# One copy moved to ScalarE, a new order of attention units between half output steps, and partial sums in buffers of their own

## The chip, the cores and the metric

The program runs on one core of a Trainium2 chip. The metric is the device time of one execution in microseconds (us); a profile's span, from its first to its last instruction, is about 1.8 us shorter. The machine prints with every execution the mean clock that was granted to TensorE. Here that number matters more than usual: executions of one and the same kernel fall into a group at a mean clock of 0.998 to 1.000, called full-clock or fast below, and one at 0.966 to 0.993, called slow. Comparisons of kernels below are between full-clock executions, where a kernel has any. Where a recorded ratio includes a lower clock, this is said, and the ratio without it, a plain ratio of mean times, is given beside it. That the slow group is made by these kernels themselves is shown by experiments that provoke it (5: a gap of 3.40 us, four of four executions at a clock of 0.966 to 0.986) and remove it (6: the gap filled, six of six at 0.998 to 1.000).

## The reference

Per head, an 8x8 matrix P is made from `sort_net` by five rounds of exp, row and column normalisation. P mixes the blocks of k and of v, attention runs inside each block of 96 rows, and the result goes through a bilinear FFN.

```python
k_sorted = einsum('bhij,bhjcd->bhicd', P, k_b)        # 4 x 8 heads, 8 blocks of 96, D = 64
v_sorted = einsum('bhij,bhjcd->bhicd', P, v_b)
scores = scale * q_b @ k_sb.T
attn = exp(scores - max); attn /= attn.sum(-1) + 1e-9
x = (attn @ v_sb) as (3072, 512)
out = ((x @ w_a) * (x @ w_b)) @ w_out                 # d_ff = 1536
```

## The kernel before

Heads are handled in pairs, four pairs to a batch; g counts the pairs. "c" mixes k and v of a pair, "s" makes its scores, "o" its outputs. These units of batch b+1 are spread between the FFN steps of batch b. The prologue does the first halves of batch 0 alone. These are the parts that the argument touches (cuts marked `...`):

```python
load_q(0); make_identity(...); load_q(1)              # all of these are issued by GpSimd, in this order
for hp in range(HP): load_pair(0, hp)
load_ab(0); load_ab(1)                                # weights
...
replicate(nc.vector, 0)                               # p_rep: P repeated along the row, first half
replicate(nc.gpsimd, 1)                               # second half: behind the loads above on GpSimd
to_columns(0)                                         # TensorE: p_rep -> pc_ps
spread(...); spread(...)
load_ab(2); load_ab(3)
half_mix(0, 0, "k", "act", fill=2, cols=256)          # fill: dummy matmuls that keep TensorE busy
half_mix(0, 0, "v", "dve")
to_columns(1)                                         # needs the second half of p_rep
half_mix(0, 1, "k", "act")
...
begun = [psF.tile([P, 512], FP32, tag="F", name="pf") for _ in range(3)]
two = psA.tile([P, 2, 512], FP32, tag="A", name="two")
begun += [two[:, 0], two[:, 1]]                       # five partial FFN sums, two of them in one tile
...
def o_(g):
    stage_o(g); to_xT(g)
    if 2 * HP <= g + 2 < B * HP:
        pair_q(g + 2); stage_q(g + 2)                 # GpSimd copy, then a transposing DMA
for n in range(HP + 1):                               # order c0 s0 c1 s1 o0 c2 s2 o1 c3 s3 o2 o3
    if n < HP: us.append(c_(g0 + n)); us.append(s_(g0 + n))
    if n > 0:  us.append(o_(g0 + n - 1))
...
steps = [(1, f) for f in ab] + [(2, f) for f in po]   # an output step: 12 matmuls, weight 2
```

The softmax here doesn't subtract the row's maximum and nothing guards it: scores larger than these inputs give would overflow.

## Time and profile before

| | |
|---|---|
| time, three executions | 252.80, 252.12, 252.27 us |
| span of the profiled execution, mean clock | 251.9 us, 0.973 |
| TensorE busy, share of the chain that ended last | 241.9 us, 89% |

The page of before: first the header, then busy time and share of TensorE, then the clock granted in 40 slices of 6.3 us, in tenths.

```profile
span 251.9 us, 5520 instructions
PEclk9965799999999999999999999999999999999999
```

The third to fifth slices are the only ones below full clock. The view by windows of 1 us shows it in detail; its columns are the window, its length, then busy time with counts of PE (TensorE's matmuls), PEld (its weight loads), DVE (VectorE), ACT (ScalarE) and POOL (GpSimd), then the granted clock, and last the DMA share and GB/s.

```profile
13.00:14.00 1.00, 0.00 (x0) 0.00 (x0) 0.42 (x1) 0.15 (x1) 0.78 (x2) 1.00 1.31 206
14.00:15.00 1.00, 0.09 (x3) 0.09 (x4) 0.00 (x0) 0.00 (x0) 1.00 (x3) 0.78 1.33 199
15.00:16.00 1.00, 1.00 (x24) 0.78 (x24) 0.42 (x1) 0.30 (x1) 0.90 (x2) 0.50 1.36 196
28.00:29.00 1.00, 1.00 (x10) 0.57 (x8) 0.00 (x0) 0.00 (x0) 0.70 (x1) 0.90 1.45 196
```

TensorE does nothing from 13 to 14 us, and its clock is halved just after. The clock record of the trace has a low stretch of 13.65 us there. Why TensorE stands still is in the timeline (start, length, engine, line, operation, count, and in brackets the idle time before it and what ended it). TensorE of before:

```profile
12.26 0.38 PE L180 MATMUL mixh<-s_all,k 128*64 128x64 bf16 x12
12.44 0.38 PE L180 MATMUL mixh<-s_all,v 128*64 128x64 bf16 x12
14.91 0.28 PE L441 MATMUL pc_ps<-ident,p_rep 32*128 32x32 bf16 x4 [2.09 <-POOL p_rep L435]
15.13 0.54 PE L180 MATMUL mixh<-s_all,k 128*64 128x64 bf16 x12
...
32.80 0.32 PE L332 MATMUL two<-xT,w_a_sb 128*128 128x384 bf16 x1 [0.60 <-DVE hT L353]
...
77.28 0.34 PE L302 MATMUL sc<-qTf,kT 64*128 64x96 bf16 x8 [0.65 <-ACT kT L162]
77.80 0.35 PE L302 MATMUL sc<-qTf,kT 64*128 64x96 bf16 x8 [0.17 <-ACT vT L162]
84.71 0.65 PE L231 MATMUL o_ps<-vs,eT 96*128 96x65 bf16 x16 [0.79 <-DMA vs<-vT]
```

GpSimd of before, which TensorE waits for at 14.91:

```profile
9.80 0.71 POOL L95 DMA_DIRECT2D v<-in_v_dram  x1 [1.64 <-DMA q_first<-in_q_dram]
...
13.71 0.74 POOL L106 DMA_DIRECT2D w_b_sb<-in_moe_w_b_dram  x1 [0.22 <-issue]
14.45 0.41 POOL L435 COPY p_rep<-p_fin 32x256 f32<-32x256 f32 x1
```

The p_rep copy takes 0.41 us, but it stands in line behind DMA issues. The twelve mixing matmuls at 15.13 take 0.54 us where the same number took 0.38 at 12.26: that is the half clock. The other waits of TensorE are small: one at 32.80 for VectorE's reading of the other half of "two", and three in batch 0's output steps at 77 to 85 us.

### The profile page before, as it was taken

Reading aid. Unit: us, or ns where it says so; the run is one execution under the profiler, and the core shown is the slowest. Engines: PE = TensorE matmul, PEld = TensorE weight load, DVE = VectorE, ACT = ScalarE, POOL = GpSimd, SP = SyncE. Lnnn points to the kernel's source line nnn. Section 1 sums busy time; section 2 is a strip of 40 time slices with the busy share of each in tenths; the row PEclk is TensorE's granted clock in tenths of the full one; section 3 lists DMA queues with packets and bytes.
Section 4 is the critical chain, followed back from the end, with each engine's and each line's share of the span. In section 5 each row is a group of like instructions: output and inputs, shape, how many; then the busy total and the mean of one; then the engine's idle time right before and its main releaser. Section 6 shows DMA issues by size and latency. Waiting matters only on the chain.

```text
span 251.9 us, 5520 instructions
## 1 busy us (share of the span) xinstructions
PE 241.9 (96%) x2258; PEld 140.3 (56%) x2258; DVE 109.7 (44%) x259; ACT 104.3 (41%) x203; POOL 60.9 (24%) x88
## 2 busy tenths in 40 slices
PE   7869999999998899999999999999999999999995
PEld 2446566666654446565654456565655455666443
DVE  6735355754742424454543324363624244444110
ACT  3534475366445016555543045636342033333101
POOL 8686468610205103505051012510000000000000
PEclk9965799999999999999999999999999999999999
DMA  6999999944497997666668768645223410000123
GB/s 82 199 199 197 196 201 182 192 69 23 85 150 130 191 169 122 84 110 97 104 99 183 156 142 134 109 76 62 54 54 113 141 61 0 0 3 1 42 94 114
DMA packets 53129, 27.82 MB, mean 110 GB/s; under 512 B 29936, under 2 KB 50160, under 8 KB 53104
## 3 DMA queue, kind: packets, MB, share of 16 engines
q0 software_dynamic: 20944, 14.16, 40.1%
q1 hardware_dynamic: 32016, 13.25, 24.6%
q8 instruction: 17, 0.28, 0.5%
q10 hardware_dynamic: 144, 0.07, 0.1%
q14 instruction: 8, 0.07, 0.1%
HBM read 28.32 MB, written 6.29 MB: 137 GB/s over the span
## 4 chain that ended last, share of the span: by engine, by line
PE 89%; DMA 6%; POOL 2%; DVE 1%; ACT 0%; issue 0%
PE pf L332 50%; PE po L375 22%; PE mix L281 4%; PE o_ps L231 3%; DMA k<-in_k_dram 3%; DMA vs<-vT 3%; PE sc L302 2%; PE mixh L180 2%; PE vs_ps L208 1%; PE sc L195 1%; PE po L362 1%; PE xt_ps L222 1%; PE mixh L168 1%; PE two L332 1%; PE q_ps L260 1%
## 5 line engine op out<-in xcount | busy, mean ns | idle before, releaser
L353 DVE TENSOR_TENSOR hT<-a_sb,pf 128x384 bf16<-128x384 bf16 x95 | 52.6, 554 | 74.3 <-PE pf L332 48.4
L332 PE MATMUL pf<-xT,w_a_sb 128*128 128x384 bf16 x380 | 78.3, 328 | 0.0
L332 PE MATMUL pf<-xT,w_b_sb 128*128 128x384 bf16 x380 | 77.8, 327 | 0.0
L352 ACT CAST a_sb<-pf 128x384 bf16<-128x384 f32 x95 | 45.5, 479 | 62.1 <-PE pf L332 40.8
L375 PE MATMUL po<-w_out_sb,hT 128*128 128x512 bf16 x276 | 61.7, 379 | 0.0
L332 PEld LDWEIGHTS <-w_b_sb 128*128 128x128 bf16 x384 | 37.7, 98 | 25.5 <-DMA w_b_sb<-in_moe_w_b_dram 0.6
L332 PEld LDWEIGHTS <-w_a_sb 128*128 128x128 bf16 x384 | 35.0, 98 | 22.4 <-issue 0.3
L375 PEld LDWEIGHTS <-hT 128*128 128x128 bf16 x276 | 26.3, 98 | 30.3
L162 ACT COPY o_sb<-po 128x512 f32<-128x512 f32 (+1 forms) x13 | 7.5, 578 | 51.0 <-PE po L375 49.5
L164 DVE COPY o_sb<-po 128x512 f32<-128x512 f32 (+1 forms) x12 | 7.9, 658 | 44.3 <-PE po L375 38.7
L307 ACT ACTIVATE eT<-sc 96x768 bf16<-96x768 f32 x24 | 18.1, 803 | 3.2 <-PE sc L302 3.2
L533 POOL COPY gate<-kT 1x1 bf16<-1x1 bf16 x8 | 1.4, 180 | 72.8 <-ACT kT L162 72.8
L237 DVE TENSOR_TENSOR xp<-o_ps,rec 96x512 bf16<-96x512 f32 x24 | 15.7, 683 | 0.2
L162 ACT CAST kT<-mix 128x384 bf16<-128x384 f32 x24 | 10.3, 483 | 8.1 <-PE mix L281 8.1
L231 PEld LDWEIGHTS <-eT 96*128 96x128 bf16 x256 | 11.1, 102 | 3.7 <-issue 1.3
L95 POOL DMA_DIRECT2D v<-in_v_dram x16 | 11.5, 718 | 5.5 <-DMA w_b_sb<-in_moe_w_b_dram 2.5
L231 PE MATMUL o_ps<-vs,eT 96*128 96x65 bf16 x256 | 12.0, 199 | 0.8 <-DMA vs<-vT 0.8
L95 POOL DMA_DIRECT2D k<-in_k_dram x16 | 11.6, 724 | 4.5 <-PE pf L332 2.3
L246 POOL COPY qc<-q 128x768 bf16<-128x768 bf16 x9 | 7.5, 831 | 16.9 <-DMA q<-in_q_dram 16.9
L95 POOL DMA_DIRECT2D q<-in_q_dram x12 | 8.6, 713 | 1.4 <-DMA w_b_sb<-in_moe_w_b_dram 0.6
L164 DVE CAST vT<-mix 128x384 bf16<-128x384 f32 x12 | 6.7, 558 | 3.8 <-PE mix L281 3.8
L168 PE MATMUL heat<-warm 128*128 128x512 bf16 x21 | 6.9, 467 | 1.3 <-DVE warm L77 1.3
(80 smaller groups left out, 159.2 us busy)
## 6 DMA issues: line engine op xcount, KB each, us to landing
out_dram<-o_sb SPq DMA_DIRECT2D x17, 256.0 KB, 2.0
k<-in_k_dram POOLq DMA_DIRECT2D x16, 192.0 KB, 5.0
v<-in_v_dram POOLq DMA_DIRECT2D x16, 192.0 KB, 6.7
q<-in_q_dram POOLq DMA_DIRECT2D x12, 192.0 KB, 6.3
w_a_sb<-in_moe_w_a_dram POOLq DMA_DIRECT2D x6, 256.0 KB, 10.1
w_b_sb<-in_moe_w_b_dram POOLq DMA_DIRECT2D x6, 256.0 KB, 11.2
w_out_sb<-in_moe_w_out_dram POOLq DMA_DIRECT2D x3, 512.0 KB, 10.3
out_dram<-o_sb SPq DMA_DIRECT2D x12, 128.0 KB, 2.4
```

Of the source, the lines that this page charges most:

```text
L95: nc.gpsimd.dma_start(out=to, in_=_ap(t, base, [[W, P], [S * D, 2], [1, W]]))
L162: nc.scalar.copy(out=out, in_=in_)
L164: nc.vector.tensor_copy(out=out, in_=in_)
L168: nc.tensor.matmul(ps[:, 0:cols], lhsT=warm[:, 0:P], rhs=warm[:, 0:cols], start=True, stop=True)
L231: nc.tensor.matmul(o_ps[:, e, i * (D + 1):(i + 1) * (D + 1)], lhsT=eT[:, hf, e, i * BLK:i * BLK + P], rhs=vs[0:BLK, i0 + i, V0 - 1 + e * ( ...
L237: nc.vector.tensor_tensor(out=_ap(xp, i0 * 2 * D, [[nxp * 2 * D, BLK], [D, 2], [2 * D, NBH], [1, D]]), in0=_ap(o_ps, 1, [[1024, BLK], [511 ...
L281: nc.tensor.matmul(mix[e * D:(e + 1) * D, c // 3, c % 3 * P:(c % 3 + 1) * P], lhsT=src2[:, e, c * D:(c + 1) * D], rhs=s_all[:, 2 * g + e], ...
L307: nc.scalar.activation(out=eT[:, hf, :, 0:HB], in_=sc[0:BLK, :, 0:HB], func=AF.Exp, scale=float(scale))
L332: nc.tensor.matmul(pf[:, 0:HW], lhsT=w_sb[:, kc, m * P:(m + 1) * P], rhs=x_cols(b, kc, t), start=(kc == 0), stop=(kc == KA - 1))
L352: nc.scalar.copy(out=a_sb, in_=pf[:, 0:HW])
L353: nc.vector.tensor_mul(out=hT[:, m, t * HW:(t + 1) * HW], in0=a_sb, in1=ab[1][:, 0:HW])
L375: nc.tensor.matmul(po, lhsT=hT[:, m, c * P:(c + 1) * P], rhs=w_out_sb[:, m, :], start=(m == 0), stop=(m == KO - 1))
```

## The change

Its intent: take the copy out of GpSimd's line; let no two units share an FFN step by cutting an output step in halves; give the transposing DMA of v more time by mixing a pair before the output of the pair two back; stage q of the next pair at the scores, because the new order would leave too little time otherwise; and end the false sharing of "two". The core of the diff (cuts marked):

```diff
-            replicate(nc.vector, 0)
-            replicate(nc.gpsimd, 1)
+            replicate("dve", 0)
+            replicate("act", 1)
...
-            two = psA.tile([P, 2, 512], FP32, tag="A", name="two")
-            begun += [two[:, 0], two[:, 1]]
+            begun += [psA.tile([P, 2, 512], FP32, tag="A", name="two")[:, 0] for _ in range(2)]
...
     def ffn_out(b, c):
...
+        def part(n):
+            if n == 0:
+                held["po"] = psF.tile([P, DMODEL], FP32, tag="F", name="po")
+            for m in range(n * KO // 2, (n + 1) * KO // 2):
+                nc.tensor.matmul(held["po"], lhsT=hTs[b][:, m, c * P:(c + 1) * P],
+                                 rhs=w_out_sb[:, m, :], start=(m == 0), stop=(m == KO - 1))
+            if n == 1:
+                store(b, c, held["po"])
+        return [lambda: part(0), lambda: part(1)]
...
             def s_(g):
...
+                if 2 * HP <= g + 1 < B * HP:
+                    pair_q(g + 1)
+                    stage_q(g + 1)
             def o_(g):
                 stage_o(g)
                 to_xT(g)
-                if 2 * HP <= g + 2 < B * HP:
-                    pair_q(g + 2)
-                    stage_q(g + 2)
...
+            for u, n in ((c_, 0), (s_, 0), (c_, 1), (s_, 1), (c_, 2), (o_, 0), (s_, 2), (c_, 3),
+                         (o_, 1), (s_, 3), (o_, 2), (o_, 3)):
+                us.append(lambda u=u, g=g0 + n: u(g))
...
-            steps = [(1, f) for f in ab] + [(2, f) for f in po]
+            steps = ab + po
```

More of the change, by code (lines that the diff above doesn't have):

```diff
@@ L369, in ffn_out, with store @@
         if b == B - 1 and c == NCH - 1:
-            ffn_last(b, c)
-            return
-        hT = hTs[b]
-        po = psF.tile([P, DMODEL], FP32, tag="F", name="po")
-        for m in range(KO):
-            nc.tensor.matmul(po, lhsT=hT[:, m, c * P:(c + 1) * P], rhs=w_out_sb[:, m, :],
-                             start=(m == 0), stop=(m == KO - 1))
+            return [lambda: ffn_last(b, c)]
+        held = {}
+        def part(n):
[7 more added lines that the diff above has]
+        return [lambda: part(0), lambda: part(1)]
+    def store(b, c, po):
         o_sb = ffp.tile([P, DMODEL], FP32, tag="o_sb", name="o_sb", bufs=3)
@@ L434, in replicate @@
             def replicate(eng, hf):
-                eng.tensor_copy(
-                    out=p_rep[:, hf * NR:(hf + 1) * NR],
-                    in_=_ap(p_fin, hf * NR, [[NB * NB, BH], [1, NR], [0, CG // 2]]))
+                copy(eng, p_rep[:, hf * NR:(hf + 1) * NR],
+                     _ap(p_fin, hf * NR, [[NB * NB, BH], [1, NR], [0, CG // 2]]))
             def to_columns(hf):
@@ L545, in o_ @@
                 to_xT(g)
-                if 2 * HP <= g + 2 < B * HP:
-                    pair_q(g + 2)
-                    stage_q(g + 2)
-            for n in range(HP + 1):
-                if n < HP:
-                    us.append(lambda g=g0 + n: c_(g))
-                    us.append(lambda g=g0 + n: s_(g))
-                if n > 0:
-                    us.append(lambda g=g0 + n - 1: o_(g))
+            for u, n in ((c_, 0), (s_, 0), (c_, 1), (s_, 1), (c_, 2), (o_, 0), (s_, 2), (c_, 3),
+                         (o_, 1), (s_, 3), (o_, 2), (o_, 3)):
+                us.append(lambda u=u, g=g0 + n: u(g))
             return us
@@ L567, in paced @@
         def paced(ab, po, units, spare):
-            steps = [(1, f) for f in ab] + [(2, f) for f in po]
-            total = sum(t for t, f in steps) - 2 * spare
-            now = done = 0
-            for t, step in steps:
+            steps = ab + po
+            total = len(steps) - 2 * spare
+            done = 0
+            for now, step in enumerate(steps, 1):
                 step()
-                now += t
                 while done < len(units) and done * total < now * len(units):
@@ L585 @@
                   for m in range(KO) for t in range(2) if b > 0 or t == 1]
-            po = [lambda c=c, b=b: ffn_out(b, c) for c in range(NCH)]
+            po = [f for c in range(NCH) for f in ffn_out(b, c)]
             paced(ab, po, units_full(b + 1) if b + 1 < B else [], 3 if b == 0 else 2)
```

## The prediction

> **What bounds the kernel.** The page has TensorE busy for 241.9 of 251.9 us, and 89% of the chain that ended last. From 34 us the timeline shows groups at their repeating pace (8 matmuls of 128x384 in 1.30 us, 12 of 128x512 in 2.59 us) with almost nothing between. To win: its idle time and slow clock:
>
> 1. At 12.82 us TensorE stops for 2.09 us until GpSimd's p_rep copy lands. The copy takes 0.41 us, but GpSimd starts it at 14.45, behind four weight-load issues; p_fin was done at 11.23.
> 2. The windows view gives a granted clock of 0.50 from 14.6 to 28.2 us. Twelve mixing matmuls take 0.46 us there, 0.24 us at full clock. [...] the gap as cause is inference.
> 3. At 32.2 us, 0.60 us: the last matmul of begun[4] waits for VectorE's read of begun[3], in the same tile "two".
> 4. In batch 0's output stage two units share one step: scores follow their mix at once (0.65 + 0.17 us waiting for kT and vT copies), and the last o waits 0.79 us for vs<-vT, 6.8 us in landing.
> Batches 1 and 2 show no TensorE idle.
>
> **What the change does.**
> - Replication on ScalarE: it is free from 11.62 us (after two qT copies) until 12.67. A 256-column copy is about 0.40 us (estimate from 479 ns for 384 columns). Ready near 12.05, before TensorE asks at 12.82. Gap 1 goes: -2.1 us, all on the chain; k of pair 1 had landed at 12.47.
> - Clock: [...] Stepping through the prologue at full clock with the trace's durations (last v near 17.4, ScalarE and VectorE about 2 us a pair), the FFN starts near 21 us instead of 26.6. If the clock drops later anyway, near 23-24. Extra gain 0 to 4 us; I take 2.3.
> - Own buffers: -0.6 us. The next scores tile takes begun[3]'s buffer, free by then.
> - Half-output steps and new order: in batch 0 no two units share a step; the last mix moves from the first output step to the eleventh of twelve a/b steps, so vs has about 9 us. -1.6 us. Batches 1 and 2 keep the same pacing: about 0.
> - q staged one pair ahead instead of two: about 8 us for a 0.83 us copy and a 2.8 us transpose: 0.
>
> Sum: 2.1 + 2.3 + 0.6 + 1.6 = 6.6, less 0.4 for new small waits: 6.2 us.
>
> **Prediction: 246.1 us, 8 in 10 between 243.5 and 248.8.** Faster by over 2% (below 247.2): 0.66; within 2%: 0.33; slower: 0.01.
>
> **What would show each step.** Timeline: p_rep on ACT ending near 12.1, no gap before the second pc_ps group, first pf matmul at 21 to 24 us. Windows: [...] at best no 0.50 at all. No wait of begun[4] on hT. At 70-85 us no TensorE wait on kT, vT or vs. Batches 1 to 3 of equal length.
>
> **What would make it wrong.** The clock falling anyway: [...] then 248-249. [...] Or late weights, q copies blocking the GpSimd or SyncE queue, psA waits between c and o.

## The result, and the profile after

| | executions, us | median |
|---|---|---|
| before, first three | 252.80, 252.12, 252.27 | |
| before, three beside the kernel after | 246.99, 247.71, 247.06 | 249.92 of all six |
| after, six | 245.78, 246.03, 246.22, 245.48, 245.97, 246.53 | 246.00 |

Ratios are the mean time of one kernel's fast runs over that of the other's of the same rounds, so not quite the ratio of the medians. Here that is 0.9949, 95% interval 0.9925 to 0.9974: half a per cent, the same at the 2% mark. The forecast of the absolute time, 246.1, was hit; the forecast of the change was not. The kernel before has executions near 247.2 too, and the prediction had been reckoned from one near 252.3. The hit is luck in part: from before's slow mean (252.40) to its fast mean (247.25) it is 5.1 us, where the prediction put 4.4 on gap and clock, and from there to after 1.25 us, where it put 1.8 on the rest. The two errors nearly cancel.

The page of after has no slice below full clock:

```profile
span 244.0 us, 5508 instructions
PEclk9999999999999999999999999999999999999999
```

TensorE of after, at the places shown of before:

```profile
12.15 0.38 PE L180 MATMUL mixh<-s_all,k 128*64 128x64 bf16 x12
12.34 0.38 PE L180 MATMUL mixh<-s_all,v 128*64 128x64 bf16 x12
12.66 0.26 PE L448 MATMUL pc_ps<-ident,p_rep 32*128 32x32 bf16 x4
12.85 0.38 PE L180 MATMUL mixh<-s_all,k 128*64 128x64 bf16 x12
...
17.12 0.30 PE L195 MATMUL sc<-qT,kT 64*128 64x96 bf16 x6
18.24 0.22 PE L195 MATMUL sc<-qT,kT 64*128 64x96 bf16 x2 [0.82 <-issue]
...
26.20 0.34 PE L332 MATMUL two<-xT,w_a_sb 128*128 128x384 bf16 x1
...
70.08 0.72 PE L302 MATMUL sc<-qTf,kT 64*128 64x96 bf16 x16
75.72 0.42 PE L231 MATMUL o_ps<-vs,eT 96*128 96x65 bf16 x8 [0.17 <-DVE xp L237]
```

ScalarE of after, with the copy that GpSimd did:

```profile
11.18 0.40 ACT L162 COPY p_rep<-p_fin 32x256 f32<-32x256 f32 x1
```

The gap is gone, the wait at "two" is gone (26.20 has no bracket), and of the waits at 77 to 85 us one of 0.17 us is left, of another kind. One thing is new: at 18.24 TensorE has stood still for 0.82 us, and "issue" means that the profile shows nothing it waited for.

The comparison that counts is with a full-clock execution of before. The kernel before was therefore run again and profiled (experiment 1); its TensorE at the same places:

```profile
13.50 0.26 PE L441 MATMUL pc_ps<-ident,p_rep 32*128 32x32 bf16 x4 [0.66 <-POOL p_rep L435]
...
18.50 0.22 PE L195 MATMUL sc<-qT,kT 64*128 64x96 bf16 x2 [0.23 <-issue]
...
27.14 0.32 PE L332 MATMUL two<-xT,w_a_sb 128*128 128x384 bf16 x1 [0.61 <-DVE hT L353]
...
71.63 0.34 PE L302 MATMUL sc<-qTf,kT 64*128 64x96 bf16 x8 [0.65 <-ACT kT L162]
72.14 0.35 PE L302 MATMUL sc<-qTf,kT 64*128 64x96 bf16 x8 [0.17 <-ACT vT L162]
72.64 2.54 PE L375 MATMUL po<-w_out_sb,hT 128*128 128x512 bf16 x11 [0.16 <-issue]
78.43 0.65 PE L231 MATMUL o_ps<-vs,eT 96*128 96x65 bf16 x16 [0.17 <-DMA vs<-vT]
```

In this execution the gap is 0.66 us instead of 2.09, and the wait for vs is 0.17 instead of 0.79. Its GpSimd shows why the gap is shorter:

```profile
8.38 0.71 POOL L95 DMA_DIRECT2D v<-in_v_dram  x1 [0.23 <-DMA q_first<-in_q_dram]
...
13.04 0.41 POOL L435 COPY p_rep<-p_fin 32x256 f32<-32x256 f32 x1
```

The v load was held up for 0.23 us, not 1.64, and everything that GpSimd does after it, the copy included, comes 1.4 us earlier. The packet records of the traces fit this: each load ends with sixteen 4-byte packets. For the second q load these lie within 0.4 us of each other in the fast execution. In the slow one fifteen come by 6.60 us after the first issue and the last at 7.96; the v load that waits for q starts 8.55 us after that issue, behind the last packet, and every later load up to 10 us has its last one behind in the same way. Why one of the sixteen trails in some executions stays open.

From the two fast traces the 1.6 us between the spans (245.6 and 244.0) divide as follows:

| stretch | before, fast | after | difference |
|---|---|---|---|
| start of the span to the first FFN matmul | 21.71 us | 21.45 us | -0.26 |
| from there to the first mix of batch 1's stage | 66.38 us | 64.98 us | -1.40, of which "two" 0.61 |
| from there to the end | 157.5 us | 157.5 us | 0.0 |

### The profile page after: what moved, and what is told of

The parts are those of the page before. It is cut to its first block, busy times and chain, and to the rows that moved or that the text cites. A ratio compares the mean times of both kernels' runs of the same rounds, so it can differ in the third digit from the quotient of the medians.

```text
span 244.0 us, 5508 instructions
## 1 busy us (share of the span) xinstructions
PE 236.7 (97%) x2246; PEld 137.3 (56%) x2258; DVE 109.6 (45%) x259; ACT 104.6 (43%) x204; POOL 60.6 (25%) x87
## 4 chain that ended last, share of the span: by engine, by line
PE 94%; DVE 3%; issue 1%; ACT 1%
PE pf L332 52%; PE po L377 24%; PE mix L281 4%; PE o_ps L231 3%; PE sc L302 2%; PE heat L168 2%; PE mixh L180 2%; PE po L362 1%; PE vs_ps L208 1%; PE sc L195 1%; PE xt_ps L222 1%; PE q_ps L260 1%; PE two L332 1%; DVE xp L237 1%; DVE o_sb L164 0%
## 5 line engine op out<-in xcount | busy, mean ns | idle before, releaser
L231 PEld LDWEIGHTS <-eT 96*128 96x128 bf16 x256 | 10.3, 97 | 3.2 <-DVE xp L237 0.6
L235 DVE RECIPROCAL rec<-o_ps 96x8 f32<-96x8 f32 x32 | 5.6, 189 | 14.0 <-PE o_ps L231 14.0
L231 PE MATMUL o_ps<-vs,eT 96*128 96x65 bf16 x256 | 11.3, 193 | 0.2 <-DVE xp L237 0.2
```

What stands on the lines that cost most here:

```text
L231: nc.tensor.matmul(o_ps[:, e, i * (D + 1):(i + 1) * (D + 1)], lhsT=eT[:, hf, e, i * BLK:i * BLK + P], rhs=vs[0:BLK, i0 + i, V0 - 1 + e * ( ...
```

## The experiments

All gave correct results. Each job also ran the kernel before in the same rounds. Jobs, each on another chip: experiments 1 to 4, 5 to 8, 9 to 12, 13 to 15.

**1. The kernel before, again.** No edit. Theory A puts the low clock of some executions down to the 2.09 us gap.

> The kernel before, unchanged, to find what its two groups of times (246.99 to 247.71 and 252.12 to 252.8 us) are. Theory A [...]: both groups can appear; an execution near 247 has a granted clock of 1.00 through 14 to 28 us although the gap of about 2 us is still there, and one near 252 or more has about 13.6 us of half clock. Theory B (a slower chip or session, nothing to do with the gap): all runs of this job lie in one group and the kernel after, or parts of it, are slow with it. Under A a fast profile has a span near 245 us and starts its FFN near 22 to 22.5 us.

Measured: five executions, 247.19 to 247.63 us, clock 0.999 to 1.000. Beside it, before ran 12 times on the same chip: nine at 246.88 to 247.59 (clock 0.999 or 1.000) and three at 252.13 to 253.34 (clock 0.973 to 0.980). Both groups come on one chip in one job, which theory B does not allow. The FFN starts at 21.71, a little earlier than expected. The gap is there, but it is not "about 2 us": it is 0.66, so the expectation was wrong in this, and the two profiled executions differ in the gap itself.

**2. Only the replication on ScalarE.**

```diff
-            replicate(nc.gpsimd, 1)
+            replicate("act", 1)
```

> Before plus only the replication on ScalarE. Theory A: no execution of the slow group; clock 1.00 throughout; p_rep on ACT done before 12 us and no gap. Theory A1 (the gap counts in full at full clock too): 245.0 us, 2.1 below the fast runs of before. Theory A2 (at full clock the prologue after the gap is bound by arriving v and weights and by ScalarE and VectorE, so the gap is mostly hidden): 246.5 to 247.3, under 0.6 below the fast runs of before. Theory B: as often slow as before.

Measured: 246.65 to 248.57 us, six executions, all at full clock; ratio 1.0011 (0.9987 to 1.0035). No slow one, as theory A says. The gap is gone in the trace and yet there is no gain over before's fast runs, so theory A1 falls. A2 is nearer, but four of the six executions lie above its range, and the cause that it names is not what the traces show in the end (below). The executions lie in groups at 246.7, 247.7 and 248.6; the profiled one is of the lowest, 246.70.

**3. The kernel after, with the replication back on GpSimd.**

```diff
-            replicate("act", 1)
+            replicate(nc.gpsimd, 1)
```

> The kernel after with the replication back on GpSimd. Theory A: the gap is back, so executions in a slow group 5 to 6 us above its fast ones may appear; its fast ones under A1 at 248.1 (after plus 2.1), under A2 at 246.0 to 246.5. Theory B: no slow group unless all kernels of the job are slow.

Measured: four of seven at full clock, 245.75 to 246.89 us; three at 250.65 to 250.97 with clock 0.973 to 0.979. The profile caught a slow one: a gap of 2.04 us and 10.24 us of half clock from 14.8 us. With GpSimd back the slow group is back. The fast executions are as fast as after's, so the gap again costs little at full clock.

**4. Only the half steps, the new order and the staging of q.** The parts of the diff from `ffn_out` on.

> Before plus the split output steps, the new order of units and the staging of q at the scores; tile 'two' and GpSimd replication as before. From the traces of before and after, batch 0 from the first FFN matmul is 1.35 us shorter by this part: fast runs 245.5 to 245.9, and in the trace no TensorE wait of more than 0.2 us between 65 and 80 us. If the gain is lost in waits elsewhere: 246.5 to 247.1. Slow executions under theory A as in before.

Measured: four fast at 246.35 to 246.39 us, one slow at 251.73; ratio 0.9965 (0.9952 to 0.9979), so about 0.9 us. From the first FFN matmul to batch 1's first mix it takes 65.66 us against 66.38, so 0.72 us and not 1.35. The 1.35 had come from the slow trace, whose wait for vs was longer; the largest wait left between 65 and 80 us is 0.18 us.

**5. The gap made long in every execution.** Two dummy copies on GpSimd ahead of the replication.

```diff
+            nc.gpsimd.tensor_copy(out=w_out_sb[:, 8:10], in_=_ap(warm, 0, [[512, P], [0, 2], [1, 512]]))
+            nc.gpsimd.tensor_copy(out=w_out_sb[:, 10, 0:256], in_=warm[:, 0:256])
             replicate(nc.gpsimd, 1)
```

> Before, with two dummy GpSimd copies (about 1.4 us together, estimate from 0.83 us for a 768-column copy) ahead of the GpSimd replication, so that the gap is about 2.1 us in every execution and not only where the second q load lands late. Theory A (the idle gap lets the clock fall): all or nearly all executions slow, 251.5 to 254 us, with 10 to 14 us of half clock from about 14.6 us. Theory C (the late load itself, or something that comes with it, lowers the clock, and the gap is a bystander): mostly 248.5 to 249, clock 1.00, and slow only as often as before (3 of 12).

Measured: 254.34, 251.38, 255.00 and 254.37 us, clock 0.966 to 0.986 in all four. The profile:

```profile
16.31 0.28 PE L441 MATMUL pc_ps<-ident,p_rep 32*128 32x32 bf16 x4 [3.40 <-POOL p_rep L435]
```

The gap was 3.40 us, since this execution also had the late q load, and 13.65 us of half clock follow it. Before kept its clock in five of 11 executions of this job, this kernel in none of four.

**6. The gap filled with dummy matmuls.** The copy stays on GpSimd, as late as it is.

```diff
             half_mix(0, 0, "v", "dve")
+            keep_busy(heat[:, 0], 8)
             to_columns(1)
```

> Before, with 8 dummy matmuls of 512 columns (1.73 us at full clock, from 0.216 us each) put into the gap ahead of the second pc_ps group; GpSimd still replicates, as late as ever. Theory A: no slow execution at all; executions with the early q load 0.6 to 1.1 us over before's fast ones (248.0 to 248.5), those with the late load 0.3 to 1.4 over (247.7 to 248.8); clock 1.00. Theory C: still slow executions near 252 to 254.

Measured: 248.07 to 249.46 us, six executions, none slow, clock 0.998 to 1.000. Its profile is one with the late q load, and its p_rep copy starts at 14.30 us:

```profile
13.21 1.90 PE L168 MATMUL heat<-warm 128*128 128x512 bf16 x8
15.05 0.26 PE L441 MATMUL pc_ps<-ident,p_rep 32*128 32x32 bf16 x4
```

A late load, a late copy, no idle TensorE, and no loss of clock. With experiment 5 this settles theory A against theory C: here it is TensorE's idleness that costs the clock, and not the late load.

**7. After, with q staged behind o again.**

```diff
             def s_(g):
-                if 2 * HP <= g + 1 < B * HP:
-                    pair_q(g + 1)
-                    stage_q(g + 1)
             def o_(g):
+                if 2 * HP <= g + 2 < B * HP:
+                    pair_q(g + 2)
+                    stage_q(g + 2)
```

> The kernel after with only the staging of q put back behind o, two pairs ahead. In the new order o of a pair comes right before the scores two pairs on, so q of those scores is asked for one FFN step (about 1.4 us) or two before it is used, against 0.83 us copy plus 2.8 us transpose. If the move was needed: TensorE waits on qTf of 1 to 3 us at up to 8 places, 250 to 256 us. If other slack covers it: 245.8 to 246.5.

Measured: 257.60 to 260.44 us, worse than expected. The profile has four waits, and with three of them goes a stretch of 3.41 us at half clock:

```profile
113.82 0.81 PE L302 MATMUL sc<-qTf,kT 64*128 64x96 bf16 x16 [2.25 <-DMA qTf<-qc]
130.33 0.52 PE L302 MATMUL sc<-qTf,kT 64*128 64x96 bf16 x16 [2.48 <-DMA qTf<-qc]
177.07 0.51 PE L302 MATMUL sc<-qTf,kT 64*128 64x96 bf16 x16 [2.80 <-DMA qTf<-qc]
191.43 0.52 PE L302 MATMUL sc<-qTf,kT 64*128 64x96 bf16 x16 [1.96 <-DMA qTf<-qc]
```

The low stretches begin at 113.87, 130.94 and 192.38 us. The longest wait, 2.80 us, is the one without, so the length of a wait alone does not decide. The stretches in the clock records of the traces have lengths that are multiples of 3.413 us: 3.41 here, 10.24 in experiment 3, 13.65 and 225.28 in before, 238.93 in after; that the clock goes in such steps is my estimate from these lengths. Counted in such steps from the end of the second low stretch, that wait is the only one that a step's border (175.31 us) cuts into 1.04 and 1.76 us; the other three lie each within one step.

So the move of the staging gains nothing by itself, but the new order can't do without it.

**8. The kernel after, again.** No edit.

> The kernel after, unchanged, beside before on one chip. Theory A: no slow execution in any round, 245.4 to 246.6, clock 1.00, whatever before does; over all executions the mean gain is the fast gain of about 1.3 us plus about 5 us times before's share of slow executions. Whether the spread of 1 us is again the late q load (the second q landing 7.0 instead of 5.6 us after its issue) the trace may show if it catches one.

Measured: 245.43 to 246.54 us, six executions, all at full clock. Before, beside it: five of 11 at full clock (247.14 to 247.87), one at 249.37 with clock 0.986, five at 251.42 to 252.90. Ratio of the fast runs 0.9927 (0.9889 to 0.9965); this set of before includes the one at 249.37. Without it the ratio is 0.9942, which agrees with the first result. The profiled execution (246.54) had an early q load; its p_fin came 0.70 us later than in the first profile of after (245.78), so nearly all of the 0.76 us between the two comes from the end of the softmax chain and not from q.

**9. Only the two buffers.**

```diff
-            two = psA.tile([P, 2, 512], FP32, tag="A", name="two")
-            begun += [two[:, 0], two[:, 1]]
+            begun += [psA.tile([P, 2, 512], FP32, tag="A", name="two")[:, 0] for _ in range(2)]
```

> Before plus only the two partial tiles in buffers of their own. The 0.61 us wait of the last begun[4] matmul on the hT product goes, in early and late executions alike: fast executions 246.7 to 246.9 beside 247.3 of before, slow ones still there at 251.5 to 253 as often as before. If the wait only moves to the next scores tile: 247.3.

Measured: three fast at 246.69 to 246.84, as expected; three slow at 250.85 to 251.75. Ratio 0.9963 (0.9937 to 0.9990). The profile is of a slow one with an early q load and a gap of only 0.96 us:

```profile
13.68 0.26 PE L441 MATMUL pc_ps<-ident,p_rep 32*128 32x32 bf16 x4 [0.96 <-POOL p_rep L435]
```

So a gap of 0.96 us can be enough, where 0.66 and 0.75 us (experiments 1 and 4) were not. Where the gap lies bears on this too. In steps of 3.413 us (the estimate of experiment 7), counted back from the fall, the step before the fall is 11.34 to 14.75 us; it holds the whole gap, and TensorE was busy in it for 2.23 us. In experiments 1 and 4 the step with the gap had 2.75 and 2.67 us busy. Over the prologues of all profiles with a clock record, the clock fell after the steps with 0.02 to 2.23 us busy and after none with 2.5 us or more. That is no general rule: in experiment 7 a step amid FFN matmuls with 1.65 us busy (175.31 to 178.72) kept the clock. No experiment moved the steps against a fixed gap.

**10. Only the output steps in halves, with their pacing; old order.**

> Before plus only the output steps in halves with their pacing; order of units and staging of q as before. By the trace of before's fast execution the waits of scores on kT and vT (0.65, 0.17 and 0.16 us) come from two units in one step; they go with the split alone, so fast executions 246.3 to 246.7, as good as split, new order and q staging together (246.37). If the new order is what gains: 247.0 to 247.4, with a wait of o on vs<-vT of 1 us or more.

Measured: fast 247.36 to 247.42; three others at 249.48 to 253.88 with clock 0.971 to 0.986. No gain: the main expectation was wrong, and its alternative, 247.0 to 247.4 with a longer wait for vs, came true. The profile is of a slow execution; set beside the slow one of before, the waits of the scores on kT and vT are gone, but the last o waits 1.39 us where it waited 0.79:

```profile
83.64 0.65 PE L231 MATMUL o_ps<-vs,eT 96*128 96x65 bf16 x16 [1.39 <-DMA vs<-vT]
```

Half steps, new order and staging of q belong together: the half steps alone gain nothing (10), and the new order without the staging loses some 12 us (7). The new order without the half steps was not run.

**11. Only the replication, once more.** As experiment 2.

> The replication alone once more, for the two groups within its fast executions (246.65 to 246.70 and 247.66 to 248.57). Theory D: the groups are the early and the late second q load; [...] and its FFN starts about 1 us later than 21.2 us at clock 1.00. Theory E: the groups come from something else (the start of the softmax chain, instruction fetch); a profile near 247.7 then shows the load complete early.

Measured: 246.83 to 247.41 us, six executions, all at full clock; ratio 0.9976 (0.9955 to 0.9997). The profile caught a late q load, but by 0.46 us only, and its FFN starts at 21.70 us against 21.18 in experiment 2. Of these 0.52 us, 0.36 are a longer stall (0.92 against 0.56 us, see below) and 0.10 a later p_fin, so theory D, by which the load makes the groups, is not shown. The group at 247.7 of experiment 2 was not seen again, and what made it stays open.

**12. After, without three filler matmuls.**

```diff
-            half_mix(0, 2, "k", "act", fill=1)
+            half_mix(0, 2, "k", "act")
```

The same for "k" and "v" of pair 3.

> The kernel after without the three single filler matmuls in the mixes of pairs 2 and 3 (0.32, 0.32 and 0.22 us on the chain of after's profile). If the prologue's own matmuls keep the clock up: 245.2 to 245.7, 0.3 to 0.8 below after. If the fillers carry the clock: some or all executions with half clock, 249 to 251.

Measured: 245.44 and 245.45 at full clock, 246.49, 247.00 and 248.25 at 0.986 to 0.993, and one of 612.94. The fillers do carry the clock in part, and the version is no better. The one of 613 us was the profiled one. Its matmuls are twice as long as after's (326 ns) from beginning to end:

```profile
L332 PE MATMUL pf<-xT,w_b_sb 128*128 128x384 bf16 x380 | 192.7, 684 | 0.0
```

Its slow matmuls begin with the first one, ahead of the first filler taken out, which speaks against the edit as their cause; what was stays open. The record gives its clock as 1.0, but the trace of this execution has no clock record. It is left out of every comparison.

By now what was open was where the replication's gain goes at full clock. Six profiles that kept full clock in the prologue have a stall without releaser, always after exactly the 224th weight load: 0.23 us in experiment 1 (before), 0.56 and 0.92 in 2 and 11 (the replication alone), 0.82 and 0.81 in after and 8, 0.62 in 7. Two others, 4 and 6, have none; both still wait for GpSimd's copy or do dummy work ahead of it. So the stall is larger where the gap is gone. In experiments 2 and 11:

```profile
17.97 0.22 PE L195 MATMUL sc<-qT,kT 64*128 64x96 bf16 x2 [0.56 <-issue]
18.50 0.22 PE L195 MATMUL sc<-qT,kT 64*128 64x96 bf16 x2 [0.92 <-issue]
```

The page lists a DMA queue of the kind "instruction" (q8, 17 packets in before). In the traces the first of its packets of 16,384 bytes starts at 15.69 to 16.61 us, and the stall ends 2.2 to 2.5 us after it in all six. That TensorE waits for this packet is my estimate from these times, theory I below. Experiments 13 to 15 put more instructions ahead of the place of the stall.

**13. After, with 24 more instruction pairs at the start.** 32 warm-up matmuls of 128 columns instead of 8 of 512.

```diff
-            keep_busy(heat[:, 0], 8)
+            keep_busy(heat[:, 0], 32, 128)
```

> The kernel after, with its first 8 warm-up matmuls of 512 columns issued as 32 of 128 columns: the same columns, 24 more weight loads and matmuls ahead of everything. Theory I (the stall of 0.56 to 0.92 us that the profile gives no releaser, always after exactly the 224th weight load, is TensorE waiting for its next block of instructions): the stall is again after the 224th weight load, now in the mixes or scores 24 pairs earlier in the program, and ends about 2.2 to 2.5 us after the instruction queue's packet; the FFN may start up to 0.6 us earlier or as now, 245.4 to 246.3. Theory S (the stall belongs to the scores of pair 2, through something the profile does not show): it stays at those scores, after the 248th load, 0.6 to 0.9 us.

Measured: 244.83 to 245.62 us, four executions, clock 1.000; ratio to before 0.9901 (0.9864 to 0.9938). In this job the set of before includes one at 249.57 with clock 0.985; without it the ratio is 0.9910, so 2.2 us against the 1.3 and 1.4 us of after (the result, experiment 8). The stall is gone, at the scores and everywhere else in the prologue. The same scores of pair 2:

```profile
17.88 0.34 PE L195 MATMUL sc<-qT,kT 64*128 64x96 bf16 x8
18.16 0.40 PE L208 MATMUL vs_ps<-ident,vT 128*128 128x128 bf16 x4
```

The first packet of 16,384 bytes on the instruction queue now starts at 13.22 us instead of 15.80. Theory S, by which the stall stays with the scores, falls. Theory I as I had written it expected a stall after the 224th load again, and was wrong there: the packet started about 2.6 us earlier, and no stall followed it.

**14. After, with 40 more pairs.** `keep_busy(heat[:, 0], 48, 85)` in the same place.

> As before this one, with 48 warm-up matmuls of 85 columns: 40 more pairs. Theory I: the stall again after the 224th weight load, 40 pairs earlier in the program. Theory S: at the scores of pair 2, after the 264th. Time 245.2 to 246.5 under I, depending on whether the block is asked for earlier too.

Measured: five at 244.96 to 245.74 with clock 1.000, one at 250.19 with 0.979; ratio 0.9909 (0.9872 to 0.9946), 0.9915 without the 249.57. No stall; the packet starts at 12.13 us and the FFN at 20.63. One of six executions lost the clock, with the replication on ScalarE; it was not profiled, and its cause stays open. At 24 pairs none of four did, too few to tell the two apart.

**15. Only the replication, with the 24 pairs.**

> Before plus the replication on ScalarE, with the same 24 extra pairs. Theory I: the replication's gain of about 0.5 to 0.7 us at full clock is what the stall takes back in the unshifted kernel (ratios 1.0011 and 0.9976); if the shift shortens the stall, this one is 246.3 to 246.8, 0.5 to 0.9 below before's fast runs. Theory S: 246.8 to 247.6.

Measured: 246.18 to 246.65 us, five executions, all at full clock; ratio 0.9957 (0.9925 to 0.9989), 0.9966 without the 249.57, where the unshifted kernel had 1.0011 and 0.9976. No stall; the FFN starts at 20.69 us instead of 21.71 in before. In time this is clearly below before (all five under all its executions), but not clear of experiment 11, so the traces have to decide:

```profile
17.26 0.34 PE L195 MATMUL sc<-qT,kT 64*128 64x96 bf16 x8
17.54 0.40 PE L208 MATMUL vs_ps<-ident,vT 128*128 128x128 bf16 x4
```

From the end of p_fin to the first FFN matmul it takes 10.45 us in before (experiment 1), 10.05 and 10.47 with the replication alone (2, 11), 10.30 and 10.37 in after (the result, 8), and 9.66, 9.41 and 9.41 with the shift (13, 14, 15). Less their own stall, those of 2, 11, after and 8 are 9.48 to 9.56. So the stall accounts for what the replication did not gain, to within 0.2 us. What was not run is a change of the warm-up that leaves the start of that packet where it was.

## Why the prediction was right or wrong

- **The base, wrong.** "Sum: 2.1 + 2.3 + 0.6 + 1.6 = 6.6, less 0.4" was taken off 252.27 us. The three times and the profile at hand all belonged to the slow group, and the profile said so: clock 0.973. This is the step that failed: 4.4 of the 6.6 us, the gap and the clock, were costs of that slow execution, and against the fast executions of before the change measured 1.25 us. I read the half clock as a property of the kernel, and not of some of its executions. In the jobs, with experiment 1 counted in, before kept full clock in 36 of 52 executions.
- **"Gap 1 goes: -2.1 us, all on the chain", mis-sized.** At full clock the gap is 0.66 us (experiment 1), and taking it away alone gives 1.0011 and 0.9976 of before's time. Of what the trace frees, TensorE gives back half to all at the stall, which grows from 0.23 to 0.56 and 0.92 us. (The 1.0011 also holds the executions at 247.7 and above that stay unexplained.) That it is the wait for the packet on the instruction queue is an estimate that experiments 13 to 15 support: the packet starts at 13.22 and 12.13 us in 13 and 14, the stall is gone in all three, and the way from p_fin to the FFN takes 9.41 to 9.66 us; the profile does not name the releaser.
- **"Extra gain 0 to 4 us; I take 2.3", mis-sized for the comparison.** The gap as cause was right: a gap kept long (3.40 us in the profile) loses the clock in four of four executions (5), a filled one in none of six (6). But in fast executions there is no slow clock to win back, so this term is 0 there. What the replication does is remove the slow group: 24 executions of after and of the replication alone (experiments 2, 8, 11 and the six of the result) had none. Variants of after with it still lost some clock in three of five (12, fillers removed, the one of 613 us aside) and one of six (14), so it is no guarantee.
- **"Own buffers: -0.6 us", right.** 0.61 us in the trace, and 0.9963 alone.
- **"Half-output steps and new order ... -1.6 us", too large.** It measured 0.9 us in time and 0.72 in the trace (experiment 4). The wait for vs was 0.79 us in the slow trace and is 0.17 in the fast one, and a new wait of 0.17 us for VectorE is the price.
- **"q staged one pair ahead ... 0", right.** Without the move the kernel takes 257.6 to 260.4 us (7).
- **"the FFN starts near 21 us", "Ready near 12.05", "about 0.40 us", right or near enough.** 21.45, 11.58 and 0.40. "Batches 1 to 3 of equal length" was right too: 157.5 us in the slow trace of before and in after.

The best version is after with 24 more instruction pairs at the start: 0.9910 of before's full-clock runs, where after has 0.9949 and 0.9942. The two were not run side by side.

## What to carry to other kernels

Look at the state and clock of the profile before reckoning any gain from it, and run the kernel often enough to see all its groups; a gain that consists in winning back a low clock is not there in a fast execution (here 2.3 of the 6.6 us that were added up). A cheap copy in the line of an engine that issues DMAs can be held up with them: here it started at 14.45 us instead of 13.04 when one q load came late. Put it on an engine that is free at that time. When a wait is removed and the time stays, look further along the same engine for a stall without a releaser, and try to move it by shifting the instruction stream (here 24 more pairs at the start took a stall of 0.82 us to none, experiment 13).
